# Attention feeding routed experts on one core: row tiles of short runs transposed by DMA, those of full runs by TensorE through stage-1 buffers

## The chip, the cores and the metric

The kernel runs on one core of one Trainium2 chip. The metric is the device time of one execution in microseconds. Before the change it was 476.42 us, the median of 3 runs (475.78 to 477.98). The profile is of one execution; its span, from the first to the last instruction, is 473.8 us.

The engines are named as in the profile: PE is TensorE's matmul, PEld its weight load, DVE is VectorE, ACT is ScalarE, POOL is GpSimd, SP is SyncE. SPq, ACTq and POOLq are the queues on which these three issue DMA transfers.

## The reference

Attention with queries averaged in pairs, then one of eight two-layer experts for each row:

```python
# q, k, v: (8, 8, 1152, 64); domain_id: (4608,), values 0..7; w1: (8, 512, 1024); w2: (8, 1024, 512)
q_pool = q.reshape(B, H, S // 2, 2, D).mean(axis=3)
scores = (1 / sqrt(D)) * q_pool @ k.T
attn = softmax(scores)                       # over the 1152 keys
attn_out = attn @ v                          # (8, 8, 576, 64)
x = attn_out.transpose(0, 2, 1, 3).reshape(4608, 512)
for e in range(8):
    mask = domain_id == e
    out[mask] = maximum(x[mask] @ w1[e], 0) @ w2[e]
```

## The kernel before

**Attention.** 32 pairs of heads, 12 steps each, 384 steps. A step computes 2 x 432 columns of scores, takes their exponential on ScalarE, and multiplies earlier exponentials with v. The loop's counter is `t`; `p, s_ = divmod(t, 12)`.

```python
    for t in range(NST + 4):                  # NST = 384
        ...
        if main:
            score(t)                          # PE: s <- qz, kq
            expo(t)                           # ACT: e <- exp(s)
        if t == 0:
            rest_k()                          # chunks 2..8 of the first pair's k: transposes, copy
        if t in (1, 2, 3):
            keep_warm(3)                      # matmuls on zeros
        work_ns = C_S                         # 370; + 315 per value product, + 460 / 420 for turning k / q
        ...
```

A row of x goes to memory once the four pairs of its batch are done (`put_x`, five row blocks for each batch). Of the last batch, odd blocks are stored through ScalarE's queue and even ones through SyncE's.

**Routing.** During the attention, VectorE and TensorE work out which rows go to which expert. Every expert gets five tiles (e, 0) to (e, 4) of 128 places (CAP = 640). Tiles 0 to 2 hold only rows of earlier batches, tiles 3 and 4 may need the last one. A tile's rows are fetched by an indirect DMA of GpSimd (`get_x`, tile `xs`, 128 rows of 512 in fp16), and its results are scattered to `out` by another.

**Filling.** Some tiles are computed during the attention, in TensorE's spare time. A tile is four blocks: `turn`, two halves of the first product, the second product. Each piece has a cost in ns, and a piece is taken if `debt + work_ns + cost - STEP <= LAG` (STEP 769, LAG 190):

```python
        def turn():
            turned.append((e, i))
            mt = mpsum.tile([P, ND, P], F16, name="m")
            for cc in range(ND):              # ND = 4
                nc.tensor.transpose(mt[:, cc, :], in_=xs[e, i][:, cc * P : (cc + 1) * P], identity=ident16[:, :])
            h0["xt"] = fill.tile([P, ND, P], F16, name="xt0")
            h0["h"] = fill.tile([P, NF, P], F16, name="h0")
            nc.vector.tensor_copy(h0["xt"][:, :, :], mt[:, :, :])
        ...
        fb.blocks.append(([turn], 240, 1, False, h0))
        fb.blocks.append(([lambda f=f: up(f) for f in range(4)], 216, 1, True, h0))
        fb.blocks.append(([lambda f=f: up(f) for f in range(4, 8)], 216, 1, True, h0))
        fb.blocks.append(([lambda f=f: down(f) for f in range(NF)], 216, 1, True, h0))   # NF = 8
        # a tile's first block is taken at the earliest 14 steps after its rows were asked for
```

The list of tiles is (0,0), (1,0), (2,0), (0,1), (1,1), (2,1), (3,0), (3,1). A tile begun by the end of the attention is finished there. The weights of four experts are loaded during the attention (`wpool` has four places); the others are loaded in the tail, each when the last run of an earlier expert is done.

**Tail.** What is left is planned as runs of tiles of one expert, (expert, first tile, end):

```python
    def plan_runs():
        early = [e for e in range(3, HELD) if done.get(e, 0) < NA]        # HELD = 4, NA = 3
        runs.extend((e, done.get(e, 0), NA) for e in early)
        runs.extend((e, done.get(e, 0), NTC) for e in range(3))           # NTC = 5
        runs.extend((e, NA if e in early else done[e], NTC) for e in range(3, HELD))
        runs.extend((e, 0, NTC) for e in range(HELD, E))

    def first_xt():                           # transposes of the first run, by TensorE
        e, i0, i1 = runs[0]
        for i in range(i0, i1):
            mt = mpsum.tile([P, ND, P], F16, name="m")                    # mpsum: one tile
            ...                               # 4 transposes, then a copy by VectorE
```

Stage 1 is the first product and its relu, stage 2 the second product. The transposes of the next run stand between the tiles of stage 2:

```python
    hps: PSUM, 2 tiles "hp" of [128, 1024] fp32      ops: 2 tiles "op"      xps: 2 tiles "xp"

    def stage1(w1h, xt, m, at=None):          # m: rows of the run
        hT = tb.tile([P, NF, CAP], F16, name="hT")
        for f in range(NF):
            if m > 512:
                hp_ = hps.tile([P, 1024], FP32, name="hp")
            elif f % 2 == 0:
                hb_ = hps.tile([P, 1024], FP32, name="hp")
                hp_ = hb_[:, 0:512]
            else:
                hp_ = hb_[:, 512:1024]
            ...                               # 4 matmuls for each 512 columns
            if f % 2 == 0: nc.scalar.activation(hT[:, f, 0:m], hp_[:, 0:m], AF.Relu)
            else:          nc.vector.tensor_scalar(out=hT[:, f, 0:m], in0=hp_[:, 0:m], scalar1=0.0, scalar2=None, op0=ALU.max)

    for k_, r in enumerate(runs):
        ...                                   # fetch rows of coming runs
        h = stage1(wts[e][0], xt[k_], n * P, ...)
        btw = [lambda i=i: turn_tile(nx, xs[en, j0 + i], i) for i in range(j1 - j0)]   # next run: 4 transposes and a copy
        stage2(wts[e][1], h, n, ..., btw)
        if i1 == NTC and rest:
            ...                               # load the weights of the next expert in rest
```

Of the kernel before, what the change touches and what calls it, by code (L numbers as in the profile page):

```python
# [9 lines left out]
P = 128  # L10
# [9 lines left out]
def kernel(  # L20
# [34 lines left out]
    NFX = 20  # L55
# [4 lines left out]
    wpool = ctx.enter_context(tc.tile_pool(name="wpool", bufs=4))  # L60
# [10 lines left out]
    idp = att.enter_context(tc.tile_pool(name="idp", bufs=2))  # L71
    lop = att.enter_context(tc.tile_pool(name="lop", bufs=6))
# [21 lines left out]
    def load_q(p, gate=False):  # L94
        b, h = p // HP, 2 * (p % HP)
        q2 = lds.tile([QP, 2, NJ, 2 * D], FP32, name="q2")
        mark(q2[0:1, 0, 0, 0:1], gate)
        for lo, hi in ((0, 1), (1, 2)) if p < 2 else ((0, 2),):
            nc.sync.dma_start(
                q2[:, lo:hi, :, :].rearrange("p h j d -> p h (j d)"),  # L100
                q[b, h + lo : h + hi].rearrange("h (p r) d -> p h (r d)", p=QP),
            )
        loaded.setdefault(p, {})["q2"] = q2
# [23 lines left out]
    k32 = perm.tile([P, 2, NC, D], FP32, name="k32")  # L127
# [12 lines left out]
    load_q(1)  # L140
# [23 lines left out]

    load_v(0)
    load_k(1)
    load_dom()
    keep_warm(17)
    make_identity(nc, ident[:, :])
# [258 lines left out]
    def id_group(g, i):  # L428
        if i == 0:
            gst["eq"] = idp.tile([P, GC, NH], F16, name="eq")  # L430
            nc.vector.tensor_tensor(
                out=gst["eq"][:, :, :],
                in0=hif[:, g * GC : (g + 1) * GC].unsqueeze(2).broadcast_to([P, GC, NH]),
                in1=iol[:, 0:NH].unsqueeze(1).broadcast_to([P, GC, NH]), op=ALU.is_equal,
            )
            gst[g] = idp.tile([P, GC, 2, NH], F16, name="hi2")
        else:
            nc.vector.tensor_tensor(
                out=gst[g][:, :, i - 1, :], in0=gst["eq"][:, :, :],
                in1=dig[:, i - 1, g * GC : (g + 1) * GC].unsqueeze(2).broadcast_to([P, GC, NH]),  # L440
                op=ALU.mult,
            )

    def id_lo(c):
        gst["lo", c] = lop.tile([P, P], F16, name="lo1")
        nc.vector.tensor_scalar(
            out=gst["lo", c][:, :], in0=iol[:, :], scalar1=lof[:, c : c + 1], scalar2=None,
            op0=ALU.is_equal,
        )
# [91 lines left out]
    def new_kq(p):  # L541
        if p not in kq:
            kq[p] = work.tile([P, KW], F16, name="kq")
# [90 lines left out]
    def put_x(b, i):  # L634
        for lo, hi in zip(CUT, CUT[1:]):
            i_, m = (0, lo) if lo < 64 else (1 + (lo - 64) // P, (lo - 64) % P)
            if i_ == i:
                j, p0 = divmod(lo, QP)
                (nc.scalar if b == B - 1 and i % 2 else nc.sync).dma_start(
                    x_dram[1 : N + 1, :].rearrange("(b p j) c -> b j p c", b=B, j=NJ)[  # L640
                        b, j, p0 : p0 + hi - lo, :
                    ],
                    xb[b][m : m + hi - lo, i, :],
                )
# [15 lines left out]
    xs = {}  # L660
    wqueue = []
# [10 lines left out]
    HELD = 4  # L672
    WANT = [66, 100, 134, 230]
# [34 lines left out]
    keep_warm(6)  # L708
# [3 lines left out]
    def rest_k():  # L712
        keep_warm(2)
        kb = wps[:, 0, :].bitcast(F16)
        turn_k32(kb, CUTK, NC)
        nc.vector.tensor_copy(kq[0][:, CUTK * P : NC * P], kb[:, 0 : (NC - CUTK) * P])
        keep_warm(3)
# [23 lines left out]
    tiles, turned = [], []  # L741

    def add_tile(e, i):
# [3 lines left out]
        def turn():  # L747
            turned.append((e, i))
            mt = mpsum.tile([P, ND, P], F16, name="m")
            for cc in range(ND):  # L750
                nc.tensor.transpose(
                    mt[:, cc, :], in_=xs[e, i][:, cc * P : (cc + 1) * P], identity=ident16[:, :]
                )
            h0["xt"] = fill.tile([P, ND, P], F16, name="xt0")
            h0["h"] = fill.tile([P, NF, P], F16, name="h0")
            nc.vector.tensor_copy(h0["xt"][:, :, :], mt[:, :, :])

        def up(f):
            if f % 4 == 0:
                h0["m"] = mpsum.tile([P, 4, P], FP32, name="m")  # L760
            m = h0["m"]
            for cc in range(ND):
                nc.tensor.matmul(  # L763
                    m[:, f % 4, :], lhsT=wts[e][0][:, cc, f * P : (f + 1) * P],
                    rhs=h0["xt"][:, cc, :], start=cc == 0, stop=cc == ND - 1,
                )
            if f % 4 == 3:
                nc.vector.tensor_scalar(
                    out=h0["h"][:, f - 3 : f + 1, :], in0=m[:, :, :],
                    scalar1=0.0, scalar2=None, op0=ALU.max,  # L770
                )

        def down(f):
            if f == 0:
                h0["o"] = mpsum.tile([P, 512], FP32, name="m")
# [13 lines left out]
        fb.blocks.append(([turn], 240, 1, False, h0))  # L789
        fb.blocks.append(([lambda f=f: up(f) for f in range(4)], 216, 1, True, h0))  # L790
# [3 lines left out]
    for e, i in [(e, i) for i in range(2) for e in range(3)] + [  # L794
        (e, i) for e in range(3, HELD) for i in range(2)
    ]:
        add_tile(e, i)

    want = [(e, 0, 114) for e in range(3)] + [(e, 1, 212) for e in range(3)]
    want += [(e, i, 212) for e in range(3, E) for i in range(2)]  # L800
    want += [(e, 2, 308) for e in [3, 0, 1, 2] + list(range(HELD, E))]
# [27 lines left out]
    xt = {0: perm.tile([P, ND, CAP], F16, name="xt_first")}  # L829

    def plan_runs():
        early = [e for e in range(3, HELD) if done.get(e, 0) < NA]
        runs.extend((e, done.get(e, 0), NA) for e in early)
        runs.extend((e, done.get(e, 0), NTC) for e in range(3))
        runs.extend((e, NA if e in early else done[e], NTC) for e in range(3, HELD))
        runs.extend((e, 0, NTC) for e in range(HELD, E))

    def first_xt():
        e, i0, i1 = runs[0]
        for i in range(i0, i1):  # L840
            mt = mpsum.tile([P, ND, P], F16, name="m")
            for cc in range(ND):
                nc.tensor.transpose(
                    mt[:, cc, :], in_=xs[e, i][:, cc * P : (cc + 1) * P], identity=ident16[:, :]
                )
            nc.vector.tensor_copy(xt[0][:, :, (i - i0) * P : (i - i0 + 1) * P], mt[:, :, :])

    debt = 0
    for t in range(NST + 4):
# [17 lines left out]
        if t == 0:  # L867
            rest_k()
        if t in (1, 2, 3):
            keep_warm(3)  # L870
# [25 lines left out]
        if t == NST + 1:  # L896
            while fb.open():
                fb.piece()
            plan_runs()
            first_xt()  # L900
        if main and want and t >= want[0][2] and t >= last_get + 5 and not (t in later) and not mmq and not rq:
            e, i, _ = want[0]
            if len(got) < NFX or list(got)[len(got) - NFX] in turned:
                get_x(fxs, e, i)
                got[e, i] = last_get = t
                want.pop(0)
        while main:
            if fb.cur is None:
# [3 lines left out]
                if not b_[3] and t < got.get(b_[4]["xs"], NST) + 14:  # L912
                    break
# [50 lines left out]
    while wqueue:  # L964
# [4 lines left out]
        tc.tile_pool(name="hps", bufs=2, space=bass.MemoryType.PSUM, reuse_waits="tile")  # L969
# [4 lines left out]
    xps = ctx.enter_context(  # L974
        tc.tile_pool(name="xps", bufs=2, space=bass.MemoryType.PSUM, reuse_waits="tile")
    )
    tb = ctx.enter_context(tc.tile_pool(name="tb", bufs=2, reuse_waits="tile"))
    xsb = ctx.enter_context(tc.tile_pool(name="xsb", bufs=10, reuse_waits="tile"))
    xov = ctx.enter_context(tc.tile_pool(name="xov", bufs=1, reuse_waits="tile"))
    ob = ctx.enter_context(tc.tile_pool(name="ob", bufs=8, reuse_waits="tile"))  # L980

    def turn_tile(xt, x_, i):
        ps = xps.tile([P, ND, P], F16, name="xp")
        for cc in range(ND):
            nc.tensor.transpose(  # L985
                ps[:, cc, :], in_=x_[:, cc * P : (cc + 1) * P], identity=ident16[:, :]
            )
        if i % 2 == 0:
            nc.vector.tensor_copy(xt[:, :, i * P : (i + 1) * P], ps[:, :, :])
        else:  # L990
            nc.scalar.copy(xt[:, :, i * P : (i + 1) * P], ps[:, :, :])
# [4 lines left out]
    def stage1(w1h, xt, m, at=None):  # L996
        hT = tb.tile([P, NF, CAP], F16, name="hT")
        for f in range(NF):

            if m > 512:  # L1000
                hp_ = hps.tile([P, 1024], FP32, name="hp")
            elif f % 2 == 0:
                hb_ = hps.tile([P, 1024], FP32, name="hp")
                hp_ = hb_[:, 0:512]
            else:
                hp_ = hb_[:, 512:1024]
# [15 lines left out]
        return hT  # L1022

# [27 lines left out]
    for k_, r in enumerate(runs):  # L1051
        e, i0, i1 = r
        n = i1 - i0
        while todo and todo[0][0] <= k_ + 1:
            fetch(k_ + 1)
        if k_ == len(runs) - 1:
            nc.gpsimd.drain()
        get = lambda: fetch(k_ + 2)
        h = stage1(wts[e][0], xt[k_], n * P, {1: get, 4: get, 6: get} if n < NTC else {1: get, 3: get, 5: get})
        btw = []  # L1060
        if k_ + 1 < len(runs):
            nx = xt[k_ + 1] = new_xt()
            en, j0, j1 = runs[k_ + 1]
            btw = [lambda i=i: turn_tile(nx, xs[en, j0 + i], i) for i in range(j1 - j0)]
# [11 lines left out]
    with tc.If(anyov > 0):  # L1076
# [9 lines left out]
        for e in range(E):  # L1086
# [4 lines left out]
            with tc.For_i(0, nt, 1) as j:  # L1091
# [13 lines left out]
                turn_tile(xto, xo, 0)  # L1105
# [30 lines left out]
```

The softmax here doesn't subtract the row's maximum and nothing guards it: scores larger than these inputs give would overflow.

## Time and profile before

| What | Value |
|---|---|
| median of 3 runs | 476.42 us |
| span of the profiled execution | 473.8 us |
| PE busy | 443.1 us, 94% of the span |
| ACT busy | 348.0 us, 73% |
| DVE busy | 227.8 us, 48% |
| POOL busy | 161.4 us, 34% |
| mean granted TensorE clock | 0.992 |
| moved by DMA | 75.23 MB, mean 159 GB/s |

The span cut into 40 slices of 11.8 us shows the two stages. A digit is the busy share of a slice in tenths:

```profile
PE   7999999999999999999999999996888879999993
ACT  3999999999999999999999999991222223223220
DMA  9995699999999788599978666003219999912203
```

ScalarE is full from the second slice to the 27th: that is the attention. The rest is the experts' tail. A group of instructions is named by its line in the kernel, engine, operation, and output and input by the program's names; a number in brackets behind a row of the timeline is the idle time of the engine before it, with what ended it.

### The profile page before, as it was taken

What the parts mean: (1) busy time and instruction counts of PE and PEld (TensorE: products, weight loads), DVE (VectorE), ACT (ScalarE), POOL (GpSimd) and SP (SyncE); (2) the same over time, 40 slices, a digit from 0 to 9 for tenths busy, and PEclk for the clock granted to TensorE, in tenths of its full rate; (3) what the DMA queues carried; (4) which work ended last, traced back from release to release, by engine and by line L of the source; (5) the groups of instructions that cost most, each with busy time, mean ns of one, the idle gap of its engine ahead of it and who ended that gap; (6) DMA issues with size and microseconds to landing.
All of it is one profiled execution on the core that took longest, in us unless ns stands there. A gap on an engine that the chain in (4) does not pass through costs nothing.

```text
span 473.8 us, 13280 instructions
## 1 busy us (share of the span) xinstructions
PE 443.1 (94%) x5683; PEld 313.9 (66%) x5683; DVE 227.8 (48%) x572; ACT 348.0 (73%) x459; POOL 161.4 (34%) x271
## 2 busy tenths in 40 slices
PE   7999999999999999999999999996888879999993
PEld 4777777877877877777787787773444445555551
DVE  4488778876454554554455454433222223232230
ACT  3999999999999999999999999991222223223220
POOL 4311231222611304564512432003336675533313
PEclk9999999999999999999999999998999999999998
DMA  9995699999999788599978666003219999912203
GB/s 204 219 245 90 129 240 221 183 260 189 167 244 227 121 201 185 100 200 276 244 124 207 138 120 150 1 25 96 80 58 169 217 222 222 232 58 84 81 16 109
DMA packets 48904, 75.23 MB, mean 159 GB/s; under 512 B 5567, under 2 KB 35008, under 8 KB 48834
## 3 DMA queue, kind: packets, MB, share of 16 engines
q0 software_dynamic: 35056, 50.05, 55.2%
q1 hardware_dynamic: 13186, 23.83, 18.6%
q8 instruction: 46, 0.75, 0.7%
q10 hardware_dynamic: 592, 0.39, 0.3%
q14 instruction: 24, 0.20, 0.1%
HBM read 95.46 MB, written 15.21 MB: 234 GB/s over the span
## 4 chain that ended last, share of the span: by engine, by line
ACT 52%; PE 26%; issue 11%; POOL 6%; DMA 3%; DVE 1%; POOLq 1%; ACTq 0%
ACT e L599 49%; PE s L587 8%; PE hp L1010 5%; PE op L1031 4%; PE acc L610 4%; POOL out_dram L504 4%; DMA w2h<-in_moe_w_dram 3%; ACT hT L1015 2%; PE m L763 1%; POOL xs L648 1%; PE m L776 1%; PE tp L550 1%; PE xp L985 1%; PE tp L564 0%; PE acc L161 0%
## 5 line engine op out<-in xcount | busy, mean ns | idle before, releaser
L599 ACT ACTIVATE e<-s 128x864 f16<-128x864 f32 x384 | 305.8, 893 | 4.7 <-PE s L587 3.9
L587 PE MATMUL s<-qz,kq 128*128 128x432 f16 (+2 forms) x1152 | 202.9, 284 | 5.6 <-ACT e L599 3.7
L610 PEld LDWEIGHTS <-e 128*128 128x128 f16 x2880 | 120.6, 97 | 24.7 <-DVE xb L624 7.8
L610 PE MATMUL acc<-v,e 128*128 128x65 f16 x2880 | 134.2, 193 | 0.3 <-ACT e L599 0.3
L587 PEld LDWEIGHTS <-kq 128*128 128x128 f16 x1152 | 97.9, 97 | 30.6 <-issue 10.2
L504 POOL DMA_INDIRECT out_dram<-osb,gid x40 | 40.2, 1004 | 102.9 <-ACT osb L1037 46.4
L648 POOL DMA_INDIRECT xs<-x_tok,grow x40 | 42.1, 1053 | 73.3 <-DVE xs L92 48.7
L1010 PE MATMUL hp<-xt,w1h 128*128 128x128 f16 (+3 forms) x384 | 57.7, 303 | 8.9 <-ACT hT L1015 8.9
L112 POOL DMA_DIRECT2D vs<-in_v_dram x32 | 23.9, 745 | 116.3 <-DVE v L529 57.1
L1031 PE MATMUL op<-w2h,hT 128*128 128x512 f16 x272 | 63.4, 379 | 0.0
L1010 PEld LDWEIGHTS <-w1h 128*128 128x128 f16 x416 | 35.9, 98 | 41.2 <-issue 17.5
L1015 ACT ACTIVATE hT<-hp 128x384 f16<-128x384 f32 (+2 forms) x36 | 20.7, 574 | 49.5 <-PE hp L1010 49.4
L1017 DVE TENSOR_SCALAR hT<-hp 128x384 f16<-128x384 f32 (+2 forms) x36 | 23.8, 661 | 65.1 <-PE hp L1010 63.6
L571 DVE COPY qz<-tp 64x576 f16<-64x576 f16 x62 | 28.2, 455 | 55.1 <-PE tp L564 51.1
L1037 ACT COPY osb<-op 128x512 f32<-128x512 f32 x21 | 12.3, 586 | 55.7 <-PE op L1031 50.0
L1031 PEld LDWEIGHTS <-hT 128*128 128x128 f16 x272 | 25.4, 98 | 25.2
L623 DVE RECIPROCAL rr<-acc 128x10 f32<-128x10 f32 x32 | 7.1, 221 | 48.1 <-PE acc L610 48.0
L520 DVE TENSOR_TENSOR qp<-q 96x768 f16<-96x768 f32 x31 | 29.3, 946 | 0.0
L624 DVE TENSOR_TENSOR xb<-acc,rr 128x640 f16<-128x640 f32 x32 | 26.4, 824 | 1.1
L1039 DVE COPY osb<-op 128x512 f32<-128x512 f32 x13 | 9.0, 692 | 35.5 <-PE op L1031 26.7
L121 POOL DMA_DIRECT2D k<-in_k_dram x31 | 23.3, 752 | 6.6 <-DVE q L92 3.6
L554 DVE COPY kq<-tp 128x1024 f16<-128x1024 f16 x31 | 21.2, 684 | 2.8 <-PE tp L550 2.7
(134 smaller groups left out, 323.2 us busy)
## 6 DMA issues: line engine op xcount, KB each, us to landing
q<-in_q_dram SPq DMA_DIRECT2D x30, 576.0 KB
vs<-in_v_dram POOLq DMA_DIRECT2D x32, 288.0 KB
k<-in_k_dram POOLq DMA_DIRECT2D x31, 288.0 KB
w1h<-in_moe_w_dram POOLq DMA_DIRECT2D x16, 512.0 KB
w2h<-in_moe_w_dram POOLq DMA_DIRECT2D x16, 512.0 KB
x_tok<-xb SPq DMA_DIRECT2D x23, 96.0 KB
x_tok<-xb SPq DMA_DIRECT2D x22, 64.0 KB
q<-in_q_dram SPq DMA_DIRECT2D x4, 288.0 KB
```

What stands on the lines that cost most here:

```text
L112: nc.gpsimd.dma_start(vs[:, :, :, :], v[b, h : h + 2].rearrange("h (p c) d -> p h c d", p=P))
L504: ins = nc.gpsimd.indirect_dma_start(out=dst[:, :], out_offset=bass.IndirectOffsetOnAxis(ap=ap, axis=0), in_=src, in_offset=None, **kw,)
L520: nc.vector.tensor_tensor(out=qp[:, :, :, :].rearrange("p j h d -> p h j d"), in0=q2[:, :, :, 0:D], in1=q2[:, :, :, D : 2 * D], op=ALU.add,)
L571: nc.vector.tensor_copy(qz[p % 2][r][lo : lo + 64, :], mt[lo : lo + 64, P : P + Sp])
L587: nc.tensor.matmul(s[:, r, o : o + n], lhsT=kq[p][:, c * P : (c + 1) * P], rhs=qz[p % 2][r][:, q0 : q0 + n], start=True, stop=True,)
L599: nc.scalar.activation(e_[:, :, o : o + W], st.pop(t)[:, :, 0:W], AF.Exp, bias=0.0, scale=0.0625)
L610: nc.tensor.matmul(acc[p][:, h, i * (D + 1) : (i + 1) * (D + 1)], lhsT=e_[:, h, o + QO[i] : o + QO[i] + P], rhs=v16[p % NV][:, c, h, 0 : D ...
L624: nc.vector.tensor_tensor(out=xb[b][:, :, 2 * hp * D : 2 * (hp + 1) * D].rearrange("p i (h d) -> p h i d", h=2), in0=a[:, :, :, 0:D], in1= ...
L648: nc.gpsimd.indirect_dma_start(out=dst, out_offset=None, in_=x_dram[0 : 1 + nb * Sp, :], in_offset=bass.IndirectOffsetOnAxis(ap=ap, axis=0),)
L1010: nc.tensor.matmul(hp_[:, lo : lo + n], lhsT=w1h[:, cc, f * P : (f + 1) * P], rhs=xt[:, cc, lo : lo + n], start=cc == 0, stop=cc == ND - 1,)
L1015: nc.scalar.activation(hT[:, f, 0:m], hp_[:, 0:m], AF.Relu)
L1031: nc.tensor.matmul(op_[:, :], lhsT=hT[:, f, i * P : (i + 1) * P], rhs=w2h[:, f, :], start=f == 0, stop=f == NF - 1,)
```

## The change

It does several things together.

- The rows of a tile are transposed by a DMA that SyncE issues (`flip_x`) in the filling, for the first run, and for every run of fewer than five tiles. No TensorE instruction, PSUM tile or copy is part of it.
- Tiles of full runs of five are still transposed by TensorE, between the tiles of stage 2, but into an `hp` tile of stage 1, which is idle then. The pool `xps` goes, and `hps` has three tiles instead of two; each `f` has an `hp` tile of its own.
- `wpool` has five places instead of four. Five experts' weights are loaded in the attention; the first run is (3, 0, 3), the second (4, 0, 3). Room for it comes from fewer early row tiles (14 instead of 20) and from shared buffers.
- Of the last batch's row blocks, the odd ones are stored through GpSimd's queue and no longer ScalarE's.
- At the start, the identity is made before the first loads of v and of the second k, the q of pair 1 is asked for later, the rest of k is turned after the second step, and most matmuls on zeros behind the first step are left out.

The diff, cut to its core:

```diff
-    NFX = 20
+    NFX = 14
-    wpool = ctx.enter_context(tc.tile_pool(name="wpool", bufs=4))
+    wpool = ctx.enter_context(tc.tile_pool(name="wpool", bufs=5))
 ...
-    load_q(1)
 ...
+    keep_warm(17)
+    make_identity(nc, ident[:, :])
     load_v(0)
     load_k(1)
-    load_dom()
-    keep_warm(17)
-    make_identity(nc, ident[:, :])
 ...
-                (nc.scalar if b == B - 1 and i % 2 else nc.sync).dma_start(
+                (nc.gpsimd if b == B - 1 and i % 2 else nc.sync).dma_start(
 ...
+    def flip_x(dst, e, i):
+        nc.sync.dma_start_transpose(dst, xs[e, i][:, :])
 ...
-    HELD = 4
-    WANT = [66, 100, 134, 230]
+    HELD = 5
+    WANT = [66, 100, 134, 206, 330]
 ...
-    keep_warm(6)
+    load_q(1, True)
+    load_dom()
+    keep_warm(5)
 ...      (in rest_k: keep_warm(2) and keep_warm(3) go)
         def turn():
-            turned.append((e, i))
-            mt = mpsum.tile([P, ND, P], F16, name="m")
-            ...                               (4 transposes)
             h0["xt"] = fill.tile([P, ND, P], F16, name="xt0")
-            h0["h"] = fill.tile([P, NF, P], F16, name="h0")
-            nc.vector.tensor_copy(h0["xt"][:, :, :], mt[:, :, :])
+            flip_x(h0["xt"][:, :, :], e, i)
+            h0["t"] = now[0]
 ...
-        fb.blocks.append(([turn], 240, 1, False, h0))
-        fb.blocks.append(([lambda f=f: up(f) for f in range(4)], 216, 1, True, h0))
+        turns.append((e, i, turn))
+        fb.blocks.append(([lambda f=f: up(f) for f in range(4)], 216, 1, False, h0))
 ...
-    for e, i in [(e, i) for i in range(2) for e in range(3)] + [
-        (e, i) for e in range(3, HELD) for i in range(2)
-    ]:
+    for e, i in [(e, i) for i in range(NA) for e in range(HELD - 2)]:
         add_tile(e, i)
 ...
-        early = [e for e in range(3, HELD) if done.get(e, 0) < NA]
-        ...
+        runs.extend((e, 0, NA) for e in (HELD - 2, HELD - 1))
+        runs.extend((e, done.get(e, 0), NTC) for e in range(HELD - 2))
+        runs.extend((e, NA, NTC) for e in (HELD - 2, HELD - 1))
         runs.extend((e, 0, NTC) for e in range(HELD, E))
-    def first_xt():
-        ...
-        if t == 0:
+        if t == 1:
             rest_k()
-        if t in (1, 2, 3):
-            keep_warm(3)
 ...
+        if turns and t >= got.get(turns[0][:2], NST) + 8 and len(tiles) - len(turns) <= len(begun):
+            turns.pop(0)[2]()
+        if first and t >= got.get(first[0], NST) + 8:
+            e, i = first.pop(0)
+            turned.append((e, i))
+            flip_x(xt[0][:, :, i * P : (i + 1) * P], e, i)
 ...
-                if not b_[3] and t < got.get(b_[4]["xs"], NST) + 14:
+                if not b_[3] and t < b_[4].get("t", NST) + 6:
 ...
-        tc.tile_pool(name="hps", bufs=2, ...)
+        tc.tile_pool(name="hps", bufs=3, ...)
-    xps = ...
-    xsb = ctx.enter_context(tc.tile_pool(name="xsb", bufs=10, reuse_waits="tile"))
+    xsb = ctx.enter_context(tc.tile_pool(name="xsb", bufs=16, reuse_waits="tile"))
 ...      (stage1)
-            if m > 512:
-                hp_ = hps.tile([P, 1024], FP32, name="hp")
-            elif f % 2 == 0:
-                hb_ = hps.tile([P, 1024], FP32, name="hp")
-                hp_ = hb_[:, 0:512]
-            else:
-                hp_ = hb_[:, 512:1024]
+            hp_ = hps.tile([P, 1024], FP32, name="hp")
 ...      (the loop over runs)
+            xt[k_ + 1] = new_xt()
+            en, j0, j1 = runs[k_ + 1]
+            for j in range(j0, j1):
+                dst = xt[k_ + 1][:, :, (j - j0) * P : (j - j0 + 1) * P]
+                if j1 - j0 < NTC:
+                    flip_x(dst, en, j)
+                else:
+                    btw.append(lambda dst=dst, j=j: turn_tile(dst, xs[en, j], j))
-        get = lambda: fetch(k_ + 2)
+        get = lambda: fetch(len(runs))
```

## The prediction

> **What bounds the kernel now.** I read the per-slice page first, to split the span into stages, then the costliest groups, then the chain of waits, then the waits, the stage windows and the timeline of the stretches that the change touches.
>
> In the costliest groups, the exponential is 384 instructions of 893 ns and was kept waiting 4.7 us in all. It runs from 9.2 to 319.5 us.
>
> ```profile
> L599 ACT ACTIVATE e<-s 128x864 f16<-128x864 f32 x384 | 305.8, 893 | 4.7 <-PE s L587 3.9
> ```
>
> So up to 319.5 us ScalarE sets the pace: the chain shows four exponentials every 3.1 us, or 0.78 us a step. TensorE is nearly full too, because expert tiles are fed into its spare time. After 320 us there is no exponential, and the stage windows (columns: busy time of PE, PE weight load, VectorE, ScalarE, GpSimd with counts, granted clock, DMA share, GB/s) show who limits:
>
> ```profile
> 320.00:325.20 5.20, 2.87 (x21) 1.50 (x20) 3.02 (x8) 0.00 (x0) 1.07 (x2) 1.00 0.50 143
> 325.20:340.40 15.20, 12.89 (x68) 6.45 (x68) 3.59 (x9) 3.04 (x6) 6.02 (x11) 0.89 0.20 60
> 340.40:354.40 14.00, 11.69 (x69) 6.12 (x68) 3.58 (x9) 3.62 (x7) 5.36 (x11) 1.00 0.22 76
> 354.40:368.40 14.00, 11.69 (x69) 6.13 (x68) 3.59 (x9) 3.62 (x7) 8.49 (x15) 1.00 0.91 161
> 368.40:382.20 13.80, 11.49 (x65) 5.91 (x64) 3.25 (x8) 3.62 (x7) 8.30 (x15) 1.00 1.08 215
> 382.20:393.50 11.30, 8.89 (x69) 5.83 (x68) 3.48 (x10) 3.20 (x7) 7.89 (x13) 1.00 1.08 227
> 393.50:411.70 18.20, 18.20 (x124) 9.87 (x123) 5.67 (x11) 5.55 (x9) 10.22 (x19) 1.00 1.15 236
> ```
>
> Rows two to five are runs of three tiles, row six the run of two, row seven the first run of five. The full run keeps PE busy throughout: 18.2 us for five tiles, 3.64 each. The short runs cost 14.0/3 = 4.7 and 11.3/2 = 5.6 us a tile for the same products. The chain of waits leads here through GpSimd, but PE is the engine with no holes from 393.5 to 466.4 us, so I take TensorE's order of work as the bound of the tail, and its holes as what can be won.
>
> The holes of a short run, in the timeline of a run of three:
>
> ```profile
> 341.28 0.49 ACT L1015 ACTIVATE hT<-hp 128x384 f16<-128x384 f32 x1
> 341.82 1.46 PE L1010 MATMUL hp<-xt,w1h 128*128 128x384 f16 x8 [0.58 <-ACT hT L1015]
> 343.32 0.49 ACT L1015 ACTIVATE hT<-hp 128x384 f16<-128x384 f32 x1 [1.55 <-PE hp L1010]
> 343.86 1.46 PE L1010 MATMUL hp<-xt,w1h 128*128 128x384 f16 x8 [0.58 <-ACT hT L1015]
> ```
>
> Even and odd `f` share one `hp` tile. The odd matmuls, though they write the other half, start only once ScalarE has emptied the even half: a pair of `f` takes 2.04 us from start to start. And the join of the two stages:
>
> ```profile
> 319.80 1.89 PE L776 MATMUL m<-w2h,h 128*128 128x512 f16 x8
> ...
> 322.48 0.38 PE L843 MATMUL m<-ident,xs 128*128 128x128 f16 x4 [0.78 <-DVE osb L782]
> 322.48 0.26 PEld L843 LDWEIGHTS <-xs 128*128 128x128 f16 x4 [1.06 <-issue]
> ...
> 323.37 0.38 PE L843 MATMUL m<-ident,xs 128*128 128x128 f16 x4 [0.52 <-DVE xt_first L846]
> ...
> 325.17 0.81 PE L1010 MATMUL hp<-xt_first,w1h 128*128 128x384 f16 x4 [0.52 <-DVE xs L92]
> ```
>
> An unfinished tile's second product, then three transposes that take turns with VectorE over a single PSUM tile. The tail's first product starts at 325.17 us.
>
> **What the Trainium skill says.** "TensorE: Matmul & The Clock Gate", section "Part 4: PE-mode transpose": a TensorE transpose ends in PSUM and needs a copy afterwards. The trace agrees: every group of four is followed by a copy of 0.41 us (VectorE) or 0.59 us (ScalarE). "DMA: Bandwidth & Descriptors", section "DMA Transpose (X-bar)": the transposing DMA takes two-byte data and lands in SBUF, so no copy follows. "Advanced Engine Details and Errata", section "X-Bar Transpose (TRN2)": such transfers should be as fast as ordinary ones, 350 to 400 GB/s; a 128 KB tile would then be an estimated 0.35 us of transfer plus the fixed cost of a transfer. No run here shows it yet, and it is the weakest figure of this prediction. The clock-gate page, section "What's actually happening", says an idle TensorE falls to half clock; the trace agrees, with a granted clock of 0.89 in 325.2 to 340.4 us, and eight matmuls taking 2.72 us there against 1.46 us later.
>
> **The change, part by part.**
>
> *How many tiles the filling still does.* A tile costs 240 + 16 x 216 = 3,696 ns of the loop's budget before and 3,456 after, since the turn leaves TensorE. Adding up the budget step by step (769 per step less the attention work, lag 190) gives six tiles before, the last one with its second product after step 384; that is what the trace shows (48 matmuls of L776, the last eight at 319.8). For after it gives again six, the sixth finished at step 377; a seventh is flipped at 348 but not begun. So nine listed tiles buy no extra tile, but nothing is left over after the attention. The tail stays at 34 tiles, cut as 3, 3, 3, 3, 3, 2, 2 and three fives.
>
> *The join.* No leftover product, no transposes on PE: the first product can follow the last attention product, at 319.97 us, so at about 320.1 instead of 325.17. Saves **5.1 us**.
>
> *Separate `hp` tiles.* Three of two banks each. A run of three then needs 8 x 4 matmuls of 384 columns, at 162 ns (384 at the 2.4 columns per ns that five-tile runs show) 5.2 us, against 8 x 2.04/2 = 8.16: 2.97 a run, four runs 11.9. For the run of two, a pair repeats after 1.51 us (383.35 to 384.86) against 8 x 107 ns = 0.86: 4 x 0.65 = 2.6. Together **14.5 us**. An eviction takes 0.49 or 0.56 us, and with three tiles a matmul group waits for the one three before it, 1.3 us back; so no new wait.
>
> *Transposes off PE.* Second products start 1.95 us apart (334.80, 336.75) where eight matmuls go on for 1.73: 0.22 us a transposed tile. Of the 31 turned after the join, 15 remain (three full runs): 16 x 0.22 = **3.5 us**.
>
> *Clock.* The 2.72 against 1.46 us goes if PE never stops at the join: **1.3 us**.
>
> *The start.* The identity is made before two DMA issues of 0.90 and 0.80 us on GpSimd, for which VectorE now waits until 5.62 us; the second exponential no longer waits 1.36 us for the rest of `k`. Perhaps 1 us of these is kept, since the q of pair 1 is now asked for later and could eat it.
>
> *Weights.* A fifth place takes one load of four out of the tail. Expert 5's load is asked for when the run of expert 0 ends, about 351 us, and is needed about 388; in the trace, loads are released every 13 us (357, 370, 384), so there is slack of some 20 us. No gain of its own, since PE has no hole there now, but without it the faster tail could have met the loads.
>
> *x stores.* Four go from ScalarE's queue (2.1 us) to GpSimd's. The first gathers wait for all stores, until 327.47 us, and still will: expert 0's tiles are needed only at 320.1 + 2 x 10.4 = 341 us. Nothing on the path.
>
> Sum: 5.1 + 14.5 + 3.5 + 1.3 + 1 = 25.4 us, that is 451.0. Counting the tail anew agrees: (18.2 - 5 x 0.22)/5 = 3.42 us a tile, 34 of them 116.3, plus 15 x 0.22 = 3.3 and 0.6 of transposes crowded before the first full run, from 320.1 gives 440.3 us as PE's end against 466.4; the 7.4 us afterwards stay. I add about 2.5 us for late transposes and take **453.5 us**.
>
> **Rivals.** *One: the transposing DMA is slow or stuck.* SyncE's queue works in order, and behind a flip that waits for a gather stand q loads and stores. In the attention the loop leaves six steps, 4.7 us, between flip and first product; DMA is at a share of 0.83 to 1.05 there. If a flip landed in 8 us, six tiles would hold PE about 3 us each, some of it hidden by the scores ahead: 10 to 18 us back, about 465. In the tail a flip has a whole run, over 10 us, so only landings of many microseconds per tile hurt. For: no number in this trace. Against: 128 KB is less than a quarter of a q load (576 KB), and those come in without holding PE. *Two: weights or gathers become the bound.* With 25 us taken from PE, DMA at 1.08 to 1.15 between 368 and 412 us could hold a full run. Against: 12 MB instead of 16 MB of weights are read in the tail. If a load came 10 us late, 461. *Three: the evictions remain.* If the wait between the halves were not from the shared tile but from ScalarE's pace, 14.5 us would stay: 466. Against: full runs use one `hp` tile per `f`, and have no hole.
>
> **Range and chances.** All going well is 449 to 451; rival one or two in part 460 to 465; range **446 to 464**. Faster by over 2% means under 466.9, which even one rival alone allows: **0.89**. Within 2%: 0.07; slower, if flips hold both stages: 0.04.
>
> **What the profile after would show.** Right: PE's first tail product near 320 us, and no product between it and the attention; pairs of `f` in short runs 1.3 us apart without wait on ScalarE; second products 1.73 us apart in short runs; 34 tiles (272 matmuls) in the tail; PE's end near 440. Wrong: waits of the filling's first product or of a short run on a DMA that writes `xt0` or `xt`, exponentials waiting more than 4.7 us in all, or PE held by weights.

## The result and the profile after

The changed kernel takes 459.05 us, the median of 3 runs (458.60 to 462.05), against 476.42: a ratio of 0.9647 with a 95% interval of 0.957 to 0.972. In a later group, five runs of it beside eleven of the kernel before gave 0.9649 (0.9625 to 0.9673). The span of the profiled execution is 456.6 us. That lies within the predicted range, 5.5 us above the predicted time and 8 us above its sum of 451.0.

The exponential, in the costliest groups of the changed kernel:

```profile
L599 ACT ACTIVATE e<-s 128x864 f16<-128x864 f32 x384 | 305.9, 893 | 3.8 <-PE s L587 2.7
```

It waits 3.8 us where it waited 4.7. The filling's transposes by DMA have not held it. The last exponential ends at 317.9 us instead of 319.5. The join of the stages, in the timeline:

```profile
317.99 0.45 PE L610 MATMUL acc<-v,e 128*128 128x65 f16 x9 [0.34 <-ACT e L599]
318.27 0.81 PE L986 MATMUL hp<-xf,w1h 128*128 128x384 f16 x4
...
319.61 4.72 PE L986 MATMUL hp<-xf,w1h 128*128 128x384 f16 x28 [0.52 <-DVE xb L624]
```

The tail's first product follows the last attention product at once, with a small new wait of 0.52 us until VectorE has emptied the attention's PSUM tile. Then the runs, in the stage windows (columns as before; a run of three is 10.4 us if TensorE never stops):

```profile
318.30:329.30 11.00, 10.48 (x61) 5.37 (x58) 3.97 (x10) 2.55 (x5) 5.45 (x12) 1.00 0.52 121
329.30:343.20 13.90, 10.86 (x57) 5.47 (x57) 2.85 (x8) 3.14 (x6) 7.48 (x14) 1.00 0.62 146
343.20:354.70 11.50, 10.55 (x57) 5.40 (x56) 2.93 (x8) 3.14 (x6) 6.89 (x13) 1.00 0.49 150
354.70:365.10 10.40, 10.40 (x58) 5.48 (x56) 2.93 (x8) 3.14 (x6) 8.87 (x15) 1.00 0.85 163
365.10:376.50 11.40, 10.69 (x57) 5.47 (x56) 2.93 (x8) 3.03 (x6) 6.54 (x13) 1.00 1.16 244
376.50:385.90 9.40, 7.33 (x49) 4.50 (x47) 2.40 (x8) 2.61 (x6) 5.13 (x9) 1.00 1.28 155
...
394.30:413.60 19.30, 18.68 (x125) 9.97 (x124) 5.68 (x9) 5.55 (x9) 9.47 (x19) 1.00 0.66 169
```

Only the fourth run (354.7) is without a hole; it took 10.4 us for three tiles. The second lost 3.5 us, the sixth (two tiles, 7.0 us if whole) 2.4, the others 0.7 to 1.1 us each. What a hole looks like, in the third run's timeline:

```profile
348.45 1.67 PE L1019 MATMUL op<-w2h,hT 128*128 128x512 f16 x7
349.04 0.49 ACT L991 ACTIVATE hT<-hp 128x384 f16<-128x384 f32 x1 [1.85 <-PE hp L986]
...
350.45 3.85 SPq L663 DMA_TRANSPOSE xt<-xs  x3
350.46 0.56 DVE L993 TENSOR_SCALAR hT<-hp 128x384 f16<-128x384 f32 x1 [2.32 <-remote]
351.07 3.35 PEld L1019 LDWEIGHTS <-hT 128*128 128x128 f16 x17 [1.40 <-DVE hT L993]
351.08 3.63 PE L1019 MATMUL op<-w2h,hT 128*128 128x512 f16 x16 [0.95 <-DVE hT L993]
```

The matmuls of `f` = 7 start by 348.29 us, and stage 2's first seven follow at their usual pace. But VectorE's eviction of `f` = 7, which waits for nothing but TensorE, starts at 350.46, and SyncE's next transposes, which wait for the same matmuls, at 350.45. Elsewhere an eviction starts 0.04 us after the modelled end of its matmuls; here 1.8 us. (`remote` or `issue` in the brackets means that the profile knows no instruction whose end fits.) I call these **late evictions**. They come in five of the ten runs. In three of these, two late evictions follow each other after 1.4 us, whether the run has two tiles, three or five, though a group of matmuls then takes 0.43, 0.65 or 1.09 us (380.69 and 382.11; 349.04 and 350.46; 400.60 and 402.05). So TensorE's pace isn't what spaces them. The kernel before has none.

The trace also records, with gaps, when TensorE raises the semaphore (a counter of the chip) that an eviction waits for. As a rule that is 0.01 us after the modelled end of the matmuls. For `f` = 6 and 7 it is at 349.02 and 350.44 us, 1.05 and 1.82 us after it, and each eviction starts 0.02 us later. So it is TensorE's signal that comes late; the engines that wait for it answer at once.

The largest loss is in the second run, where the matmuls of `f` = 1 and 2 end, as modelled, at 330.81 and 331.46 us:

```profile
333.29 0.56 DVE L993 TENSOR_SCALAR hT<-hp 128x384 f16<-128x384 f32 x1 [4.77 <-issue]
333.90 0.81 PE L986 MATMUL hp<-xt,w1h 128*128 128x384 f16 x4 [1.78 <-issue]
334.74 0.49 ACT L991 ACTIVATE hT<-hp 128x384 f16<-128x384 f32 x1 [4.05 <-issue]
335.29 0.81 PE L986 MATMUL hp<-xt,w1h 128*128 128x384 f16 x4 [0.58 <-issue]
```

These two evictions are 2.5 and 3.3 us late. All three `hp` tiles are full by then, and TensorE stops until one is free.

What GpSimd does in the third run, at the time of the hole shown first:

```profile
344.53 0.99 POOL L504 DMA_INDIRECT out_dram<-osb,gid  x1 [0.23 <-issue]
...
345.82 1.00 POOL L648 DMA_INDIRECT xs<-x_tok,grow  x1 [0.23 <-issue]
...
347.12 0.96 POOL L648 DMA_INDIRECT xs<-x_tok,grow  x1 [0.23 <-issue]
...
348.43 0.95 POOL L648 DMA_INDIRECT xs<-x_tok,grow  x1 [0.26 <-DVE xs L91]
```

They end a row of six indirect transfers (from 341.89 us on) that GpSimd issues one every 1.3 us, without a pause. The other hole is at 385.95 us, where TensorE waits for the last tile that the DMA transposes:

```profile
385.95 3.67 PE L986 MATMUL hp<-xt,w1h 128*128 128x256 f16 x32 [1.25 <-SPq L1069]
```

The profile puts it down to a closing instruction of SyncE, but what landed then, at 385.91, is the transpose issued at 372.85. In the trace's packets a transposed tile is 512 packets of 256 bytes. With little else going on, the last one ends 2.0 us after the issue (1.2 us of it SyncE's own); behind weight loads it took 7.7, 10.0, 9.1 and 12.6 us.

### The profile page after: what moved, and what is told of

Same layout as the page of the kernel before. It is cut to its first block, busy times and chain, and to the rows that moved or that the text cites. A ratio compares the mean times of both kernels' runs of the same rounds, so it can differ in the third digit from the quotient of the medians.

```text
span 456.6 us, 13089 instructions
## 1 busy us (share of the span) xinstructions
PE 433.2 (95%) x5568; PEld 307.1 (67%) x5568; DVE 221.5 (49%) x558; ACT 345.8 (76%) x457; POOL 163.3 (36%) x275
## 4 chain that ended last, share of the span: by engine, by line
ACT 46%; PE 31%; issue 10%; DMA 6%; POOL 4%; DVE 1%; POOLq 1%; another core or an unknown queue 1%
ACT e L599 46%; PE s L587 11%; DMA w2h<-in_moe_w_dram 6%; PE acc L610 6%; PE hp L986 5%; PE op L1019 4%; POOL out_dram L504 3%; PE acc L160 1%; PE m L768 1%; PE m L781 1%; PE tp L550 1%; PE tp L564 0%; DVE hT L993 0%; POOLq L1046 0%
## 5 line engine op out<-in xcount | busy, mean ns | idle before, releaser
L1019 PE MATMUL op<-w2h,hT 128*128 128x512 f16 x272 | 62.1, 379 | 1.8 <-DVE hT L993 1.8
L648 POOL DMA_INDIRECT xs<-x_tok,grow x40 | 40.9, 1022 | 63.7 <-DVE xs L91 42.2
L986 PE MATMUL hp<-xt,w1h 128*128 128x384 f16 (+3 forms) x384 | 56.5, 304 | 5.6 <-issue 3.1
```

Source lines behind the costliest of these rows:

```text
L648: nc.gpsimd.indirect_dma_start(out=dst, out_offset=None, in_=x_dram[0 : 1 + nb * Sp, :], in_offset=bass.IndirectOffsetOnAxis(ap=ap, axis=0),)
L986: nc.tensor.matmul(hp_[:, lo : lo + n], lhsT=w1h[:, cc, f * P : (f + 1) * P], rhs=xt[:, cc, lo : lo + n], start=cc == 0, stop=cc == ND - 1,)
L1019: nc.tensor.matmul(op_[:, :], lhsT=hT[:, f, i * P : (i + 1) * P], rhs=w2h[:, f, :], start=f == 0, stop=f == NF - 1,)
```

## The experiments

Each ratio is to the kernel before on the same chip. Times from different groups of runs are from different chips.

**One part alone: an `hp` tile for each `f`.** The kernel before, with:

```diff
-        tc.tile_pool(name="hps", bufs=2, ...)     # and xps goes; turn_tile takes an hp tile
+        tc.tile_pool(name="hps", bufs=3, ...)
-            if m > 512: ... elif f % 2 == 0: ... else: hp_ = hb_[:, 512:1024]
+            hp_ = hps.tile([P, 1024], FP32, name="hp")
```

> The kernel before with one part of the change: an hp tile for each f, three of them, and TensorE's transposes into an hp tile. My theory, that the wait between the two halves of a shared hp tile costs 14.5 us: about 462 us, pairs of f in short runs 1.3 us apart. The rival, that ScalarE's pace sets the wait: about 476. A third theory, from the late evictions seen in the changed kernel (ScalarE and VectorE start up to 1.9 us after the modelled end of the matmuls that they wait for): they come with a denser TensorE and not with the DMA transposes, so 3 to 6 us of the 14.5 are lost here too, about 466.

Measured: 462.90 us (ratio 0.972, 0.969 to 0.976), 13.0 us less than the kernel before on that chip. Its stage windows:

```profile
325.70:336.80 11.10, 11.08 (x69) 6.16 (x69) 3.59 (x9) 3.04 (x6) 6.00 (x11) 1.00 0.29 83
336.80:347.80 11.00, 11.00 (x69) 6.12 (x68) 3.59 (x9) 3.62 (x7) 5.36 (x11) 1.00 0.29 98
347.80:358.90 11.10, 11.10 (x70) 6.19 (x69) 3.59 (x9) 3.62 (x7) 8.52 (x15) 1.00 0.82 157
```

A run of three takes 11.05 us instead of 14.0: 2.95 each, where the step said 2.97. ScalarE's pace was not the cause. Late evictions there cost no more than a hole of 0.9 us, and the next run loses 1.4 us because TensorE, which still transposes, waits for a row fetch. The clock stays at 1.00 in the first window, though the join is the old one.

**The tail's transposes back on TensorE.**

```diff
-                if j1 - j0 < NTC:
-                    flip_x(dst, en, j)
-                else:
-                    btw.append(...)
+                btw.append(lambda dst=dst, j=j: turn_tile(dst, xs[en, j], j))
```

> The changed kernel with the tail's short runs (but for the first) transposed by TensorE again, as the full runs are; the filling and the first run stay with the DMA. If the DMA transposes of the tail save 0.22 us for each of 16 tiles and cost nothing: 3.5 us slower than the changed kernel, about 462.5. If they bring about the late evictions and the wait for the last one, which landed 12.6 us after its issue: 16 x 0.22 lost and 5 to 8 us won, about 455.

460.62 us, against 458.72 of the kernel with ScalarE's stores (below) in the same group; ratios 0.967 (0.964 to 0.971) and 0.962 (0.955 to 0.968), which overlap. Late evictions are there as before, and cost it holes of up to 1.55 us. So the tail's DMA transposes don't cause them. What these save in all, 1.9 us by the medians, is not resolved here.

**Two fetches in a first stage.**

```diff
-        ... {1: get, 4: get, 6: get} if n < NTC else {1: get, 3: get, 5: get})
+        ... {1: get, 5: get})
```

> The changed kernel with two row fetches in a run's first stage and not three. The late evictions come when GpSimd has issued five or more indirect transfers one after the other. If that causes them, fewer of them in a row leave GpSimd pauses: some 3 us faster than the changed kernel, about 456. If it is a coincidence: 459 as before, with the late evictions in the same places.

A miss: 470.37 us (0.989, 0.986 to 0.992). All but one pair of late evictions were gone, but a larger wait had come:

```profile
380.75 0.59 PE L986 MATMUL hp<-xt,w1h 128*128 128x256 f16 x2 [8.57 <-DMA xt<-xs]
```

The fetches that were left over stand in GpSimd's queue behind the next weight load, so their rows, and the transposes that wait for them, come late: holes of 8.6 and 5.7 us, and two stretches of half clock (10.2 and 3.4 us). The third fetch is what brings rows in ahead of the weights.

**The last stores on ScalarE's queue again.**

```diff
-                (nc.gpsimd if b == B - 1 and i % 2 else nc.sync).dma_start(
+                (nc.scalar if b == B - 1 and i % 2 else nc.sync).dma_start(
```

> The changed kernel with the last odd row blocks stored through ScalarE's queue again. My step that the stores lie off the path: within 0.7 us of the changed kernel, 459. If ScalarE's 2 us of issuing hold the first evictions of the tail: 1 to 2 us slower. It is also a second look at the late evictions: the same places if they belong to the program, others if they are chance.

458.72 us (0.962, 0.955 to 0.968): the total can't be told from 0.965. The trace shows a cost all the same:

```profile
319.24 2.30 ACTq L639 DMA_DIRECT2D x_tok<-xb  x4
321.96 0.87 ACT L991 ACTIVATE hT<-hp 128x384 f16<-128x384 f32 x2 [4.38 <-DMA x_tok<-xb]
322.50 2.76 PE L986 MATMUL hp<-xf,w1h 128*128 128x384 f16 x16 [0.96 <-ACT hT L991]
```

ScalarE issues the stores before the tail's first eviction, whose matmuls end at 318.74 us, and TensorE waits for it: the first run takes 12.36 us, against 11.07 in the changed kernel. Late evictions come again, in the second and from the fifth to the seventh run; the first full run has none.

**No fetches in the tail** (the 18 tiles hold a constant).

```diff
-            get_x(xsb, *todo.pop(0)[1:])
+            xs[todo.pop(0)[1:]] = xno
```

> The changed kernel with the tail's 18 row fetches left out (their tiles hold a constant, so those rows of the output are not the reference's). If GpSimd's unbroken rows of indirect transfers make the evictions late: with three of six gone in each run no late evictions, and the kernel 5 to 7 us faster than the changed one, 453. If they come with TensorE's density alone: as late as before, and only the wait for the last flip may change, 458.

450.56 us (0.951, 0.947 to 0.956), no late evictions. But the next two kernels of that group had none either.

**Results stored by ScalarE, unscattered.**

```diff
-            scatter(out, osb[:, :], ids(i), "oscat", N - 1)
+            nc.scalar.dma_start(o_rows[r0 : r0 + P, :], osb[:, :])     # stage 2 only; scratch rows
```

> The changed kernel with the tail's results stored by plain transfers from ScalarE's queue into a scratch tensor, in the order of their places, instead of scattered by GpSimd into the output (those rows of the output are left out). As many bytes are moved, but GpSimd issues less. If GpSimd's rows of indirect transfers are the cause: no late evictions, 453 to 455. If it is the traffic of the transfers, or TensorE's density: late evictions remain, 458 or more, as ScalarE has 34 more issues.

453.43 us (0.960, 0.955 to 0.965), no late evictions; inconclusive because of the next one.

**The old start.** The changed kernel with the start's lines as before (identity after the first loads of GpSimd, `load_q(1)` and `load_dom()` early, `rest_k` at `t == 0`, all `keep_warm`).

> The changed kernel with the start as before: identity after the first GpSimd loads, q of pair 1 early, the rest of k turned after the first step, all matmuls on zeros. My step had about 1 us for the start; the trace shows the last exponential ending 1.5 us earlier. So 1 to 2 us slower than the changed kernel, 460.5. If the start is made good later by other waits in the attention: 459.

454.74 us (0.960, 0.955 to 0.965). Its last exponential ends at 318.97 us, against 316.76 and 316.61 of its two neighbours: the new start is worth 2.2 us there. Yet it had no late eviction with all of GpSimd's transfers in place: five short runs in a row take 10.4 us or 10.99 with the join. This is the second, in which nine indirect transfers follow each other from 326.6 us on:

```profile
330.40:340.80 10.40, 10.40 (x58) 5.51 (x57) 2.93 (x8) 3.13 (x6) 7.54 (x15) 1.00 0.90 190
```

On this chip, then, they did not occur, and on it the kernel before took 472.89 us instead of 475.3 to 476.4.

**Once more on one chip: the changed kernel, a mix, and no fetches.** The mix transposes only run (4, 3, 5) by TensorE:

```diff
-                if j1 - j0 < NTC:
+                if j1 - j0 < NTC and (en, j0) != (HELD - 1, NA):
```

> The changed kernel itself, to stand beside the other two on one chip. The late evictions were there in its first trace and in four of its relatives on one chip, but in none of three relatives on another chip, one of which (the old start) still had all of GpSimd's transfers. If they are a matter of the chip or the moment: present or absent here for all three kernels of this group alike. If of GpSimd's rows of transfers: present here, absent in the kernel without row fetches. The wait for the last transposed tile should be here in any case, 1 to 4 us. Time 0.96 to 0.965 of the kernel before.

> The changed kernel with the two tiles of run (4, 3, 5) alone transposed by TensorE, between the tiles of the run before; its DMA transposes landed 11 to 13 us after their issue, behind two weight loads, and TensorE waited 1.2 to 3.8 us for them. If that wait is on the path: it goes, and with it the 3.4 us at half clock that followed it in some traces, for 2 x 0.22 us of transposes; 1 to 4 us faster than the changed kernel. If another wait takes its place, such as for weights: the same time.

> Once more the changed kernel without the tail's 18 row fetches (left out: those rows of the output hold products of a constant). Beside the changed kernel on one chip it tells what the fetches cost in all: if they bring late evictions, 5 us or more; if late evictions are absent on this chip for all, 0 to 2 us.

The changed kernel: 459.20 us (0.9649, 0.9625 to 0.9673). Without fetches: 450.92 (0.948, 0.945 to 0.951), 8.3 us less. The mix: 458.94 (0.9634, 0.9611 to 0.9657); its wait for the last transposed tile is gone (1.8 us in the changed kernel here), but the gain can't be told from none, as late evictions took 6 to 7 us of holes in both. In the kernel without fetches, the run that answers to the one shown above:

```profile
343.75 0.49 ACT L993 ACTIVATE hT<-hp 128x384 f16<-128x384 f32 x1 [0.81 <-PE hp L988]
...
344.19 5.34 PE L1021 MATMUL op<-w2h,hT 128*128 128x512 f16 x24
344.40 0.56 DVE L995 TENSOR_SCALAR hT<-hp 128x384 f16<-128x384 f32 x1 [0.74 <-PE hp L988]
```

All 24 matmuls of stage 2 run through. Its runs of three take 10.38 us, and TensorE ends at 441.9 us against 450.2. No late eviction is left; TensorE still waits 2.0 us for the last transposed tile.

**Fetches without GpSimd, and fetches earlier.** The first issues the same number of bytes from SyncE, as 128 consecutive rows; the second moves the three fetches to `f` = 0, 1 and 3.

```diff
-            get_x(xsb, *todo.pop(0)[1:])
+            nc.sync.dma_start(x_[:, :], x_dram[r0 : r0 + P, :])        # first
-        ... {1: get, 4: get, 6: get} if n < NTC else {1: get, 3: get, 5: get})
+        ... {0: get, 1: get, 3: get})                                  # second
```

> The changed kernel with the tail's 18 row fetches issued by SyncE as plain transfers of 128 consecutive rows (as many bytes to the same tiles; the choice of rows is left out, so those rows of the output are other rows' products). If GpSimd's issuing makes the evictions late: few or none, and most of the 8 us that the kernel without fetches won, 452. If it is the traffic of the fetches: late as in the changed kernel, 458. SyncE's queue then holds fetches and transposes, and the last transposed tile may hold TensorE by 2 to 4 us.

> The changed kernel with the three row fetches of a run at f = 0, 1 and 3 instead of 1, 4 and 6. All transfers stay; GpSimd gets a pause of an estimated 2 to 3 us between the fetches and the scatters of a run (three fetches at 1.3 us end before the first result is there), so shorter unbroken rows if it keeps up. If unbroken rows bring the late evictions: fewer, 2 to 4 us faster than the changed kernel, a ratio of 0.957. If only the number of its transfers counts: the same ratio, 0.965. It also shows, beside the kernel without fetches on GpSimd, whether this chip has late evictions at all.

From SyncE: 455.38 us (0.958, 0.955 to 0.962), although the last transposed tile, 14.6 us after its issue, now holds TensorE for 4.5 us. Its first five runs are whole (11.08 with the join, then four of 10.38); the second and third in the stage windows:

```profile
328.50:338.90 10.40, 10.40 (x57) 5.48 (x56) 2.93 (x8) 3.13 (x6) 3.22 (x7) 1.00 0.81 198
338.90:349.30 10.40, 10.40 (x57) 5.46 (x56) 2.92 (x8) 3.13 (x6) 3.19 (x7) 1.00 0.53 153
```

Late evictions come only from 373 us on, by 0.5 to 0.8 us, although GpSimd had issued just three indirect transfers in a row there. Earlier fetches: 459.59 (0.966, 0.963 to 0.969), no gain. GpSimd starts late, after the last stores, and then catches up: from 325.9 us it issues nine indirect transfers without a pause, and the second run takes 18.6 us. So this edit did not make the pauses that it was to make, and says nothing against the theory; it does show that this chip has late evictions, which makes the first kernel's absence of them count.

## Why the prediction was right, and where its sum fell short

The mechanism was right: TensorE's order of work bounds the tail, and its holes were what could be won. The `hp` tiles alone make up most of the gain (ratio 0.972, against 0.965 for all parts). The join, the transposes and the start, 9.6 us in the sum, bring only some 3.6 us more by these ratios, since the losses below set in with them. The join and the weights have no run of their own; they are read from the traces.

- **Filling.** Right: 272 matmuls of stage 2, so 34 tiles in the tail, and nothing left over. Two of the six flips took 14.1 and 9.9 us to land, over the 8 us that rival one feared, and yet no product waited for one. The six steps, 4.7 us, were only the least distance: from its flip to its first product a tile had 7 us once, and 33 us or more after that. The estimate of 0.35 us for the transfer was too low: even with quiet queues the packets of a tile run for 0.8 us.
- **The join**, 5.1 us. From the last exponential to the first product it took 5.71 us before and 0.34 after, 5.4 less; 0.5 came back as the wait for the attention's PSUM tile, which the step did not see.
- **`hp` tiles**, 14.5 us. Alone they gave 13.0, and a whole run of three what was worked out. The 13.0 hold the clock's 1.3 as well: 14.5 + 1.3, less the wait of 1.4 for a row fetch, 0.9 of late evictions, and 0.5 for a first product that came later than before.
- **Transposes off TensorE**, 3.5 us. A whole run of three falls from 11.05 to 10.38 us, which is the 3 x 0.22 of the step. What remains in the whole kernel is not resolved (1.9 us by the medians, for 13 tiles).
- **Clock**, 1.3 us. The granted clock falls only after the last product now. But the step gave the join as the reason, and the trace of the `hp` tiles alone keeps the full clock with the old join. There the holes behind the join were gone and the join was not. This is one trace of each kernel.
- **The start**, 1 us: 1.5 to 2.2.
- **Weights and stores**: no product waits for weights. The stores were off the path on GpSimd's queue; in the one trace with them on ScalarE's, they lengthen the first run by 1.3 us, which the early first product has made possible.

The step that failed is a sentence under the `hp` tiles: "An eviction takes 0.49 or 0.56 us, and with three tiles a matmul group waits for the one three before it, 1.3 us back; so no new wait." The evictions do take that long, but they start late. From start to start, the runs show what this cost: 3.5 us in the second run, 1.1, 1.0 and 1.0 in the third, fifth and sixth, 0.9 in the first full run, together about 7.6. The last transposed tile cost another 1.4: rival one in small, in the tail and not in the filling. The join cost 0.7, and tiles of 3.46 us (10.38/3) instead of 3.42 cost 1.35 over 34 tiles. (The 3.42 came from a window of 18.2 us that ends before the next run starts; from start to start the full run took 18.44 before, too.) Together 11.1, less 1.8 for a first product that came earlier than 320.1: TensorE's end at 449.6 instead of 440.3. The 2.5 us that I had added were meant for late transposes alone; that the time still lies in the range is in part luck, for its width was meant for other rivals.

**What the late evictions come from** is shown so far: on a chip where the changed kernel has them, they are gone when GpSimd does not issue the tail's fetches. On another such chip they are gone from the first five runs when SyncE moves as many bytes instead. So GpSimd's part in the fetches brings them, or most of them, and not the bytes or the tail's DMA transposes. **Open** is whether it is the fetches or the sheer number of GpSimd's indirect transfers, for the kernel without its scatters ran on the one chip that had no late evictions; whether the issuing engine or the indirect form does it, for the fetches from SyncE changed both; how it holds up TensorE's signal, and whether TensorE's work ends late with it; and why one of the chips had none in three kernels. The change also lets rows be fetched any number of runs ahead, where the kernel before looked two ahead; no run takes that part alone back, though the kernel with the `hp` tiles alone still had the limit and lost only 0.9 us. A version that keeps all fetches and has no late evictions on a chip that shows them was not found.

## What to carry to other kernels

A half of a PSUM tile was no buffer in this program: two groups that shared one tile cost 0.7 us a pair, which three tiles took away as the timeline had said. Whether the chip or the program's account of its tiles made the second half wait was not tested. When the engine in the middle loses its holes, count again what the others issue in the shorter time: GpSimd's six transfers of 1.3 us are just over half of a run of 14 us and three quarters of one of 10.4. And a DMA that stands behind bulk loads needs a need date far beyond its time alone (2 us alone, up to 14.6 here), or another way.

## What the runs showed of the hardware that was not expected

- A transposing DMA of 128 x 512 fp16 from SBUF to SBUF held SyncE's queue for 1.2 us and ended 2.0 us after its issue when the queues were quiet, but 7.7 to 14.6 us after it behind weight loads in the tail, and up to 14.1 us in the attention.
- Evictions that wait only for TensorE started up to 3.3 us after the modelled end of its matmuls (3.7 in the mix, over 5 with earlier fetches). In the changed kernel they came where rows of five to seven indirect transfers by GpSimd end, and TensorE's semaphore was raised as late wherever the trace has its record. On three chips of the four in the experiments there were such evictions, on one there were none.
- The same kernel before took 472.9 us on that chip and 475.3 to 476.4 on the others.
